# Block attention and feed-forward, one core: attn*v in three steps, scores ahead of transposes, raw keys of the last blocks turned a step earlier (batches 2 to 7)

## The chip, the cores and the metric

The program runs on one core of a Trainium2 chip. The metric is device time in microseconds (us), of which three runs are given for the kernel before. The profile is of one further execution. PE is the matmul engine, PEld its weight loads, DVE the vector engine, ACT the scalar engine, POOL GpSimd, SP the engine that issues the DMAs.

## The reference

For 8 batches, 8 heads, 576 positions and head size 64, attention with a block mask (block 64: a query sees its own and all earlier blocks); then the heads side by side as 4608 tokens of 512 go through two matrices with an activation between them.

```python
scores = scale * np.matmul(q, k.transpose(0, 1, 3, 2))
scores = np.where(block_i >= block_j, scores, -1e9)
attn = softmax(scores)              # over the keys
x = (attn @ v).transpose(0, 2, 1, 3).reshape(4608, 512)
h = x @ w_in                        # 512 -> 2048
g = np.where(h >= 1, h, np.where(h <= -1, 0, (h + 1) ** 2 / 4))
out = g @ w_out                     # 2048 -> 512
```

## The kernel before

Two heads of a batch make a pair; there are 32 pairs. `attention_steps` is a generator that writes out a pair in eight steps. From the 37th step on each attention step is followed by one half step of the feed-forward part: either `ffn_in` (12 matmuls of 512 columns into the bank `ph`, then four operations on ACT, DVE and POOL) or `ffn_out` (12 matmuls of 512 columns into the four banks `po`). Odd steps of a pair are followed by `ffn_out`, even ones by `ffn_in`. When attention is through, the feed-forward half steps that are left run alone.

PE takes its instructions in the order of the program, here as a scheduler has settled it; ACT, DVE, POOL and SP each have their own order, settled in the same way.

Pairs of batches 2 to 7 (24 of the 32) are "far" and "raw" in the code: their queries and keys come as they are and are split into two parts after the transpose, and much of a pair's work is done during the next pair's steps. Short names for the groups of matmuls, each of which fills one bank:

- S(j,g): scores of head j for one or two tiles of 128 queries, with 128 and 256 keys (g=0), 384 (g=1), 512 (g=2); method `scores`, lines 482 and 485. DVE takes the negated maximum of a row (L505), ACT the exponential and its sum (L509), DVE the inverse and the product (L491, L492, L515), and a DMA (`prr<-pr`) copies the result into a tile of another type, from which PE transposes it.
- SLa, SLb: the same for the last 64 queries of both heads, two banks of 4 matmuls of 288 columns (`scores_last`).
- T(j,g): transposes of that copy (L552 before, L565 after), 3 or 4 of 128 columns; ACT copies the bank (L545), DVE subtracts the copy from it (L547). TL is the same for the last 64 queries; its last 64 keys, the corner, have a bank of their own before the change (TLb).
- Q(j): four transposes of head j's raw queries and keys (`turned_raw`, L401), taken from the bank by ACT, DVE, ACT, DVE in turn. QL: one transpose for the last blocks of both heads (`turned_last`, L442), taken by ACT, DVE, ACT, DVE and two more on DVE.
- AF: attn*v of the first 256 positions of both heads (`attn_v_first`); A(j): of the other 320 positions of head j (`attn_v`); L591 before, L608 after. ACT copies one half to `xtmp` (L613), DVE adds the halves (L614).

All of these share three banks in turn (the pool `ps_w`): a group may start when the group three places before it has been taken out of its bank. The order of the groups before the change, for the steps 1 to 8 of a pair (names of the pair before it marked with '):

```
1: T(1,1)' S(0,0) AF'   2: T(1,2)' S(0,1) QL    3: A(1)' S(0,2)    4: T(0,0) SLa SLb
5: T(0,1) S(1,0) Q(0)   6: T(0,2) S(1,1)        7: TL TLb S(1,2)   8: T(1,0) A(0) Q(1)
```

Q(0) and Q(1) are those of the next pair, QL the pair's own.

Of the kernel before, what the change touches and what calls it, by code (L numbers as in the profile page):

```python
# [23 lines left out]
def block_attn_then_ffn(  # L24
# [230 lines left out]
    class Pair:  # L255
# [238 lines left out]
        def scores(self, j, g):  # L494
# [19 lines left out]
            for i, cs in enumerate(cols):  # L514
                nc.vector.tensor_scalar_mul(pr[:, cs], pr[:, cs], sm[:, i : i + 1])  # L515
            self.pr[j, g] = as_float32r(pr[:, : cols[-1].stop], self.plain) if self.hop else [pr]

        def scores_last(self):
# [22 lines left out]
            nc.vector.tensor_scalar_mul(pr, pr, sm[:, 2:3])  # L541
            self.pr["last"] = as_float32r(pr, self.plain) if self.hop else [pr]

# [27 lines left out]

        def turn_last(self):
            pr = self.pr.pop("last")
            ps = work_bank("ps_t")
            for c0 in range(0, SM, P):
# [4 lines left out]
            )  # L580
            ps = work_bank("ps_t")
            self.transposed(ps[:BLK, :P], pr, SM, BLK)
            self.split(
                ps[:BLK, :P].rearrange("p (h c) -> p h c", h=2), *(x[:BLK] for x in self.pc)
            )

# [44 lines left out]
        def attn_v_first(self):  # L631
            if self.plain:
                return self.both(0, self.parts_first)
            ps = work_bank("ps_av")
            for j in range(2):
                self.weighted(ps[:, j * G0 : (j + 1) * G0], j, self.parts_first(j))
            for j in range(2):
                self.add_halves(ps[:, j * G0 : (j + 1) * G0], j, 0)

        def attn_v(self, j):  # L640
# [3 lines left out]
            self.weighted(ps, j, self.parts(j))  # L644
            self.add_halves(ps, j, G0)

# [16 lines left out]
    def attention_steps():  # L663
# [10 lines left out]
        for i, cur in enumerate(pairs + [None]):  # L674
            nxt = pairs[i + 1] if i + 1 < len(pairs) else None
            far = old is not None and old.far
            near = old is not None and not old.far
            if far:
                old.turn(1, 1)
            if cur:  # L680
# [13 lines left out]
            if i + 2 < len(pairs):  # L694
                pairs[i + 2].fetch()
            if near:
                old.attn_v(1)
                old.store_x()
            yield
            if far:  # L700
                old.attn_v(1)
                old.store_x()
            if not cur:
                return
            if cur.far:
                cur.scores(0, 2)
            else:
                cur.begin()
                cur.scores(0, 2)
                cur.turn(0, 0)  # L710
            yield
            if cur.far:
                cur.begin()
                cur.turn(0, 0)
                cur.scores_last()
            else:
                cur.scores_last()
                cur.turn(0, 1)
            if nxt:
# [5 lines left out]
            if cur.far:  # L725
                cur.turn(0, 1)
                cur.scores(1, 0)
            else:
                cur.scores(1, 0)
                cur.turn(0, 2)  # L730
            if nxt:
                nxt.turned(True, 0)
            yield
            if cur.far:
                cur.turn(0, 2)
                cur.scores(1, 1)
            else:
                cur.scores(1, 1)
                cur.turn_last()
            if nxt:  # L740
                nxt.turned(False, 0)
            yield
            if cur.far:
                cur.turn_last()
                cur.scores(1, 2)
            else:
                cur.scores(1, 2)
                cur.attn_v(0)
                cur.turn(1, 0)
            yield  # L750
# [134 lines left out]
```

## Time and profile before

| | |
|---|---|
| median of 3 runs | 1267.78 us (1264.84 to 1269.26) |
| the profiled execution's own time | 1269.69 us |
| its span, first to last instruction | 1267.9 us |
| mean granted clock of TensorE | 0.981 of full speed |
| PE busy | 1200.1 us, 95% of the span |
| DVE, ACT, POOL busy | 70%, 55%, 31% |

Busy time is the union of what the records of an engine cover. The ends of matmuls are modelled and overlap the next one's start, so what a matmul costs is read from one start to the next, not from its length.

### The profile page before, as it was taken

Reading aid. Unit: us, or ns where it says so; the run is one execution under the profiler, and the core shown is the slowest. Engines: PE = TensorE matmul, PEld = TensorE weight load, DVE = VectorE, ACT = ScalarE, POOL = GpSimd, SP = SyncE. Lnnn points to the kernel's source line nnn. Section 1 sums busy time; section 2 is a strip of 40 time slices with the busy share of each in tenths; the row PEclk is TensorE's granted clock in tenths of the full one; section 3 lists DMA queues with packets and bytes.
Section 4 is the critical chain, followed back from the end, with each engine's and each line's share of the span. In section 5 each row is a group of like instructions: output and inputs, shape, how many; then the busy total and the mean of one; then the engine's idle time right before and its main releaser. Section 6 shows DMA issues by size and latency. Waiting matters only on the chain.

```text
span 1267.9 us, 20253 instructions
## 1 busy us (share of the span) xinstructions
PE 1200.1 (95%) x6280; PEld 998.8 (79%) x6280; DVE 887.0 (70%) x2188; ACT 703.2 (55%) x1827; POOL 394.6 (31%) x430
## 2 busy tenths in 40 slices
PE   5888889899999999999999999999999999999998
PEld 4666667678888888888888888888888888888886
DVE  8898877758777777777777777787777777322222
ACT  5787656646566655665656655566556555222222
POOL 3555655522222222222222222222222222222222
PEclk9888988999999999999999999999999999999999
DMA  5566666667888655555554655465556433422432
GB/s 158 167 176 215 203 228 197 217 198 237 260 273 266 215 162 158 154 175 163 156 162 145 187 157 152 138 189 153 160 154 190 137 128 118 132 87 98 133 100 100
DMA packets 185259, 215.43 MB, mean 170 GB/s; under 512 B 113840, under 2 KB 132272, under 8 KB 184384
## 3 DMA queue, kind: packets, MB, share of 16 engines
q1 hardware_dynamic: 185152, 214.14, 54.9%
q8 instruction: 50, 0.82, 0.3%
q14 instruction: 57, 0.47, 0.1%
HBM read 134.74 MB, written 31.98 MB: 131 GB/s over the span
## 4 chain that ended last, share of the span: by engine, by line
PE 69%; DVE 16%; ACT 6%; issue 5%; DMA 1%; POOL 1%; SPq 1%; ACTq 0%; POOLq 0%; DVEq 0%
PE ph L770 29%; PE po L794 15%; PE po L799 7%; PE ps_av L591 7%; PE ps_s L482 4%; ACT pr L509 3%; PE ps_s L485 3%; DVE t L780 2%; PE ps_t L552 2%; DVE t L783 2%; ACT t L779 2%; DVE pb L547 2%; DVE nm L505 2%; DVE sm L491 1%; DVE pr L515 1%
## 5 line engine op out<-in xcount | busy, mean ns | idle before, releaser
L785 POOL TENSOR_TENSOR gl<-t,gh 128x512 fp32r<-128x512 f32 x144 | 187.5, 1302 | 510.2 <-ACT gh L784 333.2
L794 PE MATMUL po<-wo,gh 128*128 128x512 f32 x1152 | 296.1, 397 | 0.5 <-DMA wo<-wo_split 0.3
L794 PEld LDWEIGHTS po<-wo,gh 128*128 128x128 f32 x1152 | 212.5, 189 | 44.5 <-DMA wo<-wo_split 0.7
L770 PE MATMUL ph<-xh,wih 128*128 128x512 f32 x576 | 232.9, 404 | 1.6 <-DVE t L783 1.6
L770 PE MATMUL ph<-xh,wil 128*128 128x512 f32 x576 | 228.8, 397 | 0.0
L770 PE MATMUL ph<-xl,wih 128*128 128x512 f32 x576 | 227.8, 396 | 0.5 <-DVE xl L627 0.5
L780 DVE SCALAR_TENSOR_TENSOR t<-t 128x512 f32<-128x512 f32 x144 | 101.5, 705 | 168.0 <-ACT t L779 165.2
L779 ACT ACTIVATE t<-ph 128x512 f32<-128x512 f32 x144 | 85.9, 597 | 173.8 <-PE ph L770 173.8
L509 ACT ACTIVATE pr<-ps_s,nm 128x128 f32<-128x128 f32 (+3 forms) x256 | 134.1, 527 | 60.5 <-DVE nm L505 58.4
L784 ACT CAST gh<-t 128x512 fp32r<-128x512 f32 x144 | 89.5, 621 | 120.3 <-DVE t L783 120.0
L799 PE MATMUL po<-wo,gl 128*128 128x512 f32 x576 | 155.6, 392 | 0.0
L482 PE MATMUL ps_s<-ka,qa 68*128 68x288 f32 (+4 forms) x384 | 135.3, 367 | 15.0 <-ACT pr L509 5.4
L379 POOL TENSOR_TENSOR vsr<-vn,vsr 128x256 fp32r<-128x256 f32 (+1 forms) x96 | 55.2, 576 | 246.2 <-ACT vsr L378 244.6
L770 PEld LDWEIGHTS ph<-xh,wil 128*128 128x128 f32 x576 | 109.5, 190 | 23.8
L770 PEld LDWEIGHTS ph<-xh,wih 128*128 128x128 f32 x576 | 109.8, 191 | 21.7 <-DVE t L783 2.3
L799 PEld LDWEIGHTS po<-wo,gl 128*128 128x128 f32 x576 | 108.7, 189 | 23.1
L505 DVE TENSOR_REDUCE nm<-ps_s 128x1 f32<-128x128 f32 (+3 forms) x256 | 118.8, 482 | 10.4 <-PE ps_s L485 9.4
L770 PEld LDWEIGHTS ph<-xl,wih 128*128 128x128 f32 x576 | 109.7, 190 | 20.5 <-DVE xl L627 0.9
L485 PE MATMUL ps_s<-kb,qb 128*128 128x288 f32 (+4 forms) x384 | 121.1, 322 | 0.0
L515 DVE TENSOR_SCALAR pr<-pr,sm 128x128 f32<-128x128 f32 (+3 forms) x256 | 107.3, 440 | 5.4
L783 DVE TENSOR_TENSOR t<-ph,t 128x512 f32<-128x512 f32 x144 | 98.7, 686 | 2.2
L491 DVE TENSOR_SCALAR sm<-sm 128x1 f32<-128x1 f32 (+1 forms) x224 | 52.0, 232 | 68.3 <-ACT pr L509 65.7
(111 smaller groups left out, 1871.4 us busy)
## 6 DMA issues: line engine op xcount, KB each, us to landing
wo<-wo_split SPq DMA_DIRECT2D x144, 512.0 KB, 3.5
prr<-pr SPq DMA_DIRECT2D x96, 192.0 KB, 2.5
prr<-pr SPq DMA_DIRECT2D x72, 256.0 KB, 2.8
out_dram<-ob SPq DMA_DIRECT2D x36, 256.0 KB, 2.9
bits<-in_moe_w_in_dram SPq DMA_DIRECT2D x32, 256.0 KB, 3.5
bits<-in_moe_w_out_dram SPq DMA_DIRECT2D x32, 256.0 KB, 3.0
wo_split<-ws SPq DMA_DIRECT2D x16, 512.0 KB, 2.9
qa<-qb SPq DMA_DIRECT2D x63, 128.0 KB, 2.4
```

Source lines behind the costliest of these rows:

```text
L482: nc.tensor.matmul(ps, qa[:KA, j, c0 : c0 + P], ka[:KA, j, k0 : k0 + n], start=first, stop=False)
L485: nc.tensor.matmul(ps, qb[:, j, c0 : c0 + P], kb[:, j, k0 : k0 + n], start=False, stop=last)
L505: nc.vector.tensor_reduce(out=nm[:, i : i + 1], in_=ps[:, cs], axis=AX.X, op=ALU.max, negate=True)
L509: nc.scalar.activation(pr[:, cs], ps[:, cs], AF.Exp, bias=nm[:, i : i + 1], scale=1.0, accum_out=sm[:, i : i + 1],)
L515: nc.vector.tensor_scalar_mul(pr[:, cs], pr[:, cs], sm[:, i : i + 1])
L770: nc.tensor.matmul(ph, w[:, cc, fs], x[:, cc, xs], start=(cc == 0 and i == 0), stop=(cc == NCC - 1 and i == 2),)
L779: nc.scalar.activation(t_, ph, AF.Relu, bias=0.5, scale=0.5)
L780: nc.vector.scalar_tensor_tensor(out=t_, in0=t_, scalar=1.0, in1=t_, op0=ALU.min, op1=ALU.mult)
L783: nc.vector.tensor_tensor(out=t_, in0=ph, in1=t_, op=ALU.max)
L785: nc.gpsimd.tensor_tensor(out=gl, in0=t_, in1=gh.bitcast(F32), op=ALU.subtract)
L794: nc.tensor.matmul(po[tt], gh[:, ts_], wo[:, w, :], start=(fc == 0 and w == 0), stop=False)
L799: nc.tensor.matmul(po[tt], gl[:, ts_], wo[:, 0, :], start=False, stop=fc == NFC - 1)
```

## The change

It concerns the far pairs alone. The order of the groups becomes

```
1: S(0,0) T(1,1)' A(0)'   2: S(0,1) T(1,2)' AF'   3: S(0,2) A(1)'        4: SLa SLb T(0,0)
5: S(1,0) T(0,1) Q(0)     6: S(1,1) T(0,2)        7: S(1,2) TL Q(1)      8: T(1,0)+corner QL
```

with QL now that of the next pair. Scores stand ahead of the transposes in a step; the three parts of attn*v are spread over steps 1, 2 and 3 of the next pair; the corner is transposed into the bank of T(1,0), so a pair has 21 groups instead of 22. The DMAs `prr<-pr` are written at the end of a step (`move`). In `add_halves` both halves of AF take their columns from one `xtmp` tile.

```diff
-            self.pr[j, g] = as_float32r(pr[:, : cols[-1].stop], self.plain) if self.hop else [pr]
+            self.pr[j, g] = [pr[:, : cols[-1].stop]]
+            if not self.far:
+                self.moved(j, g)
...
+        def move(self, *key):
+
+            if self.far:
+                self.moved(*key)
...
+            if self.far and j == 1 and g == 0:
+                self.turn_corner(self.pr.pop(("last",)), ps[:BLK, n : n + P])
...
-        def add_halves(self, ps, j, c0):
+        def add_halves(self, ps, j, c0, xtmp):
...
-            xtmp = att1.tile([P, G1], F32, tag="xtmp", name="xtmp")
...
+            xtmp = att1.tile([P, G1], F32, tag="xtmp", name="xtmp")
             for j in range(2):
-                self.add_halves(ps[:, j * G0 : (j + 1) * G0], j, 0)
+                self.add_halves(ps[:, j * G0 : (j + 1) * G0], j, 0, xtmp)
...
-            if far:
-                old.turn(1, 1)
             if cur:
                 cur.scores(0, 0)
                 cur.turned(False, 1)
                 cur.load("v")
             if far:
-                old.attn_v_first()
+                old.turn(1, 1)
+                old.attn_v(0)
...
+            if cur:
+                cur.scores(0, 1)
+                if not cur.raw:
+                    cur.turned_last()
...
             if far:
                 old.turn(1, 2)
-            if cur:
-                cur.scores(0, 1)
-                cur.turned_last()
+                old.attn_v_first()
...
             if far:
+                if cur:
+                    cur.scores(0, 2)
                 old.attn_v(1)
                 old.store_x()
...
             if cur.far:
                 cur.begin()
+                cur.scores_last()
                 cur.turn(0, 0)
-                cur.scores_last()
...
-            if cur.far:
-                cur.turn(0, 1)
-                cur.scores(1, 0)
+            cur.scores(1, 0)
+            cur.turn(0, 1 if cur.far else 2)
+            cur.move(1, 0)
...
+            cur.scores(1, 1)
             if cur.far:
                 cur.turn(0, 2)
-                cur.scores(1, 1)
...
+            cur.scores(1, 2)
             if cur.far:
                 cur.turn_last()
-                cur.scores(1, 2)
+                if nxt:
+                    nxt.turned(True, 1)
...
             if cur.far:
                 cur.turn(1, 0)
-                cur.attn_v(0)
...
+            if nxt and nxt.raw:
+                nxt.turned_last()
```

The first place is PE around step 2 of a pair in the middle of the program, before the change; L799 is the end of `ffn_out`, L770 the start of `ffn_in`.

```order
L799 MATMUL po<-wo,gl 128x512 x4
L552 MATMUL ps_t<-ident_r,prr 128x128 x4
L482 MATMUL ps_s<-ka,qa 128x384
L485 MATMUL ps_s<-kb,qb 128x384
L442 MATMUL ps_qk<-ident_r,qk 128x128
L770 MATMUL ph<-xh,wih 128x512
```

The same place after the change, where L828 is the end of `ffn_out`:

```order
L828 MATMUL po<-wo,gl 128x512 x4
L482 MATMUL ps_s<-ka,qa 128x384
L485 MATMUL ps_s<-kb,qb 128x384
L565 MATMUL ps_t<-ident_r,prr 128x128 x4
L608 MATMUL ps_av<-pa_6201,vsr_111 128x256
```

The single transpose L442 (QL), which stood behind S(0,1), is gone from this place; T(1,2)' has moved behind S(0,1), and AF' follows it.

The second place is PE from step 7 to the start of step 8 before the change; L794 and L799 are `ffn_out`.

```order
L552 MATMUL ps_t<-ident_r,prr 128x128 x4
L552 MATMUL ps_t<-ident_r,prr 64x128
L482 MATMUL ps_s<-ka,qa 128x512
L485 MATMUL ps_s<-kb,qb 128x512
L794 MATMUL po<-wo,gh 128x512 x8
L799 MATMUL po<-wo,gl 128x512 x4
L552 MATMUL ps_t<-ident_r,prr 128x128 x3
```

And after the change, as far as step 8's `ffn_in`:

```order
L482 MATMUL ps_s<-ka,qa 128x512
L485 MATMUL ps_s<-kb,qb 128x512
L565 MATMUL ps_t<-ident_r,prr 128x128 x4
L401 MATMUL ps_qk<-ident_r,qk 128x128 x4
L823 MATMUL po<-wo,gh 128x512 x8
L828 MATMUL po<-wo,gl 128x512 x4
L565 MATMUL ps_t<-ident_r,prr 128x128 x3
L565 MATMUL ps_t<-ident_r,prr 64x128
L442 MATMUL ps_qk<-ident_r,qk 128x128
```

S(1,2) now stands ahead of TL, as S(1,1) in step 6 of T(0,2); the corner (64x128) has moved from step 7 to step 8, Q(1) from step 8 to step 7, and QL has come to the end of step 8.

The third place is DVE behind step 4's `ffn_in` before the change: L780 and L783 are its two operations, L505 the maxima of S(1,0), L547 the part of T(0,1), L389 that of Q(0).

```order
L780 SCALAR_TENSOR_TENSOR t<-t 128x512
L547 TENSOR_TENSOR pb_7868<-ps_t,pb_7867 128x3x128
L783 TENSOR_TENSOR t<-ph,t 128x512
L505 TENSOR_REDUCE nm<-ps_s 128x1 x2
L389 SCALAR_TENSOR_TENSOR qb<-ps_qk,qb 64x512
L491 TENSOR_SCALAR sm<-sm 128x2
L492 RECIPROCAL sm<-sm 128x2
L515 TENSOR_SCALAR pr<-pr,sm 128x128
```

And after the change, with L809 and L812 for the two operations and L560 for T(0,1):

```order
L809 SCALAR_TENSOR_TENSOR t<-t 128x512
L505 TENSOR_REDUCE nm<-ps_s 128x1
L812 TENSOR_TENSOR t<-ph,t 128x512
L505 TENSOR_REDUCE nm<-ps_s 128x1
L560 TENSOR_TENSOR pb_7440<-ps_t,pb_7439 128x3x128
L389 SCALAR_TENSOR_TENSOR qb<-ps_qk,qb 64x512
L491 TENSOR_SCALAR sm<-sm 128x2
L492 RECIPROCAL sm<-sm 128x2
```

One of the two maxima of S(1,0) now stands between the two operations of `ffn_in`, and T(0,1)'s subtraction behind the other maximum.

## Rows read from the trace of the kernel before

**Rows 1.** The page, part 2: the granted clock in 40 slices.
```profile
PEclk9888988999999999999999999999999999999999
```

**Rows 2.** One pair's period: length, PE, PEld, DVE, ACT, POOL busy (records), clock, DMA.
```profile
704.49:737.90 33.41, 32.71 (x183) 27.83 (x183) 25.78 (x64) 19.87 (x54) 9.00 (x10) 1.00 0.53 157
```

**Rows 3.** All waits of PE in 311.8 to 1080 us: total, times, longest.
```profile
PE ps_qk L442 <- DVE x L614: 8.9, 23, 0.4
PE ps_s L482 <- ACT pr L509: 5.2, 17, 0.3
```

**Rows 4.** Line 442 (QL): lengths in ns, first and last start in us.
```profile
L442 PE MATMUL ps_qk<-ident_r,qk x24: 221/252/254, 274.4 to 1047.2; 128*128 128x128 f32 x24
```

**Rows 5.** PE in order of time, steps 1 to 2: start, length, instruction.
```profile
711.83 0.41 PE L482 MATMUL ps_s<-ka,qa 68*128 68x384 f32 x1
712.08 0.34 PE L485 MATMUL ps_s<-kb,qb 128*128 128x384 f32 x1
712.83 0.25 PE L442 MATMUL ps_qk<-ident_r,qk 128*128 128x128 f32 x1 [0.41 <-DVE x L614]
712.91 0.47 PE L770 MATMUL ph<-xh,wih 128*128 128x512 f32 x1
713.22 0.39 PE L770 MATMUL ph<-xl,wih 128*128 128x512 f32 x1
713.44 0.39 PE L770 MATMUL ph<-xh,wil 128*128 128x512 f32 x1
```

**Rows 6.** DVE and ACT before that wait, in order of time.
```profile
710.35 0.41 DVE L614 TENSOR_TENSOR x<-ps_av,xtmp 64x256 f32<-64x256 f32 x1
...
711.53 0.36 ACT L613 COPY xtmp<-ps_av 64x256 f32<-64x256 f32 x1
...
712.25 0.43 DVE L614 TENSOR_TENSOR x<-ps_av,xtmp 64x256 f32<-64x256 f32 x1
```

**Rows 7.** PE in order of time, steps 5 to 7.
```profile
724.32 0.37 PE L552 MATMUL ps_t<-ident_r,prr 128*128 128x128 f32 x3
...
728.18 0.45 PE L552 MATMUL ps_t<-ident_r,prr 128*128 128x128 f32 x4
728.49 0.45 PE L482 MATMUL ps_s<-ka,qa 68*128 68x384 f32 x1
728.78 0.34 PE L485 MATMUL ps_s<-kb,qb 128*128 128x384 f32 x1
728.96 0.39 PE L770 MATMUL ph<-xh,wih 128*128 128x512 f32 x1
...
731.71 0.51 PE L552 MATMUL ps_t<-ident_r,prr 128*128 128x128 f32 x5
732.51 0.50 PE L482 MATMUL ps_s<-ka,qa 68*128 68x512 f32 x1 [0.29 <-ACT pr L509]
732.85 0.40 PE L485 MATMUL ps_s<-kb,qb 128*128 128x512 f32 x1
```

**Rows 8.** DVE and ACT in order of time behind step 4.
```profile
724.57 0.60 ACT L779 ACTIVATE t<-ph 128x512 f32<-128x512 f32 x1 [0.82 <-PE ph L770]
...
725.81 0.55 DVE L547 TENSOR_TENSOR pb<-ps_t,pb 128x384 fp32r<-128x384 f32 x1
726.28 0.68 DVE L783 TENSOR_TENSOR t<-ph,t 128x512 f32<-128x512 f32 x1
...
727.00 0.62 ACT L784 CAST gh<-t 128x512 fp32r<-128x512 f32 x1 [0.86 <-DVE t L783]
...
728.24 0.20 ACT L509 ACTIVATION_READ_ACCUMULATOR pr<-ps_s,nm 128x1 f32 x1
```

**Rows 9.** Two of DVE's groups by form, one period: busy us, mean ns.
```profile
L395 DVE TENSOR_TENSOR kb<-ps_qk,kb 64x512 fp32r<-64x512 f32 x2 | 1.4, 692 | 0.7 <-ACT kb L394 0.6
...
L446 DVE TENSOR_SCALAR ka<-ps_qk 64x128 fp32r<-64x128 f32 x1 | 0.3, 293 | 0.0
```

**Rows 10.** Line 809: DVE's copies of finished output banks, lengths in ns.
```profile
L809 DVE COPY ob<-po x18: 678/686/692, 294.0 to 1262.9; 128x512 f32<-128x512 f32 x18
```

More of the change, by code (lines that the diff above doesn't have):

```diff
@@ L541, in scores_last @@
             nc.vector.tensor_scalar_mul(pr, pr, sm[:, 2:3])
-            self.pr["last"] = as_float32r(pr, self.plain) if self.hop else [pr]
+            self.pr["last",] = [pr]
+            if not self.far:
+                self.moved("last")
         def split(self, ps, hi, lo=None):
@@ L572, in turn_last @@
         def turn_last(self):
-            pr = self.pr.pop("last")
+            pr = self.pr["last",] if self.far else self.pr.pop(("last",))
             ps = work_bank("ps_t")
@@ L580, in turn_last, with turn_corner @@
             )
[L581 to L585, printed above, removed]
+            if not self.far:
+                self.turn_corner(pr, work_bank("ps_t")[:BLK, :P])
+        def turn_corner(self, pr, ps):
+            self.transposed(ps, pr, SM, BLK)
+            self.split(ps.rearrange("p (h c) -> p h c", h=2), *(x[:BLK] for x in self.pc))
         def weighted(self, ps, j, parts, first=True, last=True):
@@ L644, in attn_v @@
             self.weighted(ps, j, self.parts(j))
-            self.add_halves(ps, j, G0)
+            self.add_halves(ps, j, G0, att1.tile([P, G1], F32, tag="xtmp", name="xtmp"))
         def store_x(self):
@@ L684, in attention_steps @@
             if far:
-                old.attn_v_first()
+                old.turn(1, 1)
+                old.attn_v(0)
             if near:
                 old.turn(1, 2)
+            if cur:
+                cur.move(0, 0)
             yield
+            if cur:
+                cur.scores(0, 1)
+                if not cur.raw:
+                    cur.turned_last()
+            if i + 2 < len(pairs):
+                pairs[i + 2].fetch()
             if far:
                 old.turn(1, 2)
-            if cur:
-                cur.scores(0, 1)
-                cur.turned_last()
-            if i + 2 < len(pairs):
-                pairs[i + 2].fetch()
+                old.attn_v_first()
             if near:
@@ L698, in attention_steps @@
                 old.store_x()
+            if cur:
+                cur.move(0, 1)
             yield
             if far:
+                if cur:
+                    cur.scores(0, 2)
                 old.attn_v(1)
                 old.store_x()
-            if not cur:
-                return
-            if cur.far:
+                if not cur:
+                    return
+                if not cur.far:
+                    cur.begin()
+                    cur.turn(0, 0)
+            elif cur.far:
                 cur.scores(0, 2)
@@ L710, in attention_steps @@
                 cur.turn(0, 0)
+            cur.move(0, 2)
             yield
@@ L718, in attention_steps @@
                 cur.turn(0, 1)
+            cur.move("last")
             if nxt:
@@ L733, in attention_steps @@
             yield
+            cur.scores(1, 1)
             if cur.far:
                 cur.turn(0, 2)
-                cur.scores(1, 1)
             else:
-                cur.scores(1, 1)
                 cur.turn_last()
+            cur.move(1, 1)
             if nxt:
@@ L742, in attention_steps @@
             yield
+            cur.scores(1, 2)
             if cur.far:
                 cur.turn_last()
-                cur.scores(1, 2)
+                if nxt:
+                    nxt.turned(True, 1)
             else:
-                cur.scores(1, 2)
                 cur.attn_v(0)
                 cur.turn(1, 0)
+            cur.move(1, 2)
             yield
@@ L756, in attention_steps @@
                 cur.attn_v_first()
-            if nxt:
+            if nxt and not cur.far:
                 nxt.turned(True, 1)
+            if nxt and nxt.raw:
+                nxt.turned_last()
             yield
```

7 lines of the change are left out of this document (3 added, 4 removed).

## The prediction

> **What bounds the kernel now.** I looked first at the granted clock: from the eighth of 40 slices on it is nine tenths or more [rows 1], and in a far pair 1.00, the upper level, 2.4 GHz [rows 2], so nothing is to be had from the clock where the change acts. Then at such a pair, one whole period: 33.41 us long, with PE covered for 32.71, DVE for 25.78, ACT for 19.87 [rows 2]. PE is the bound, and the view of waits shows what it still waits for. Between 311.8 and 1080 us there are two waits and no others: QL for DVE's addition of the halves of AF (23 times), and S(1,2) for ACT's exponential (17 times) [rows 3]. QL runs 24 times from 274.4 to 1047.2 us [rows 4], 23 periods of 33.6 us on average, so both waits repeat in nearly every pair.
>
> Because the ends of matmuls are modelled, I take each wait's cost from starts. The second matmul of S(0,1) starts at 712.08 and QL at 712.83, 0.75 us apart [rows 5]; where nothing waits, the same matmul of 384 columns takes 0.18 (728.78 to 728.96) [rows 7]. So QL's wait costs 0.57, not the recorded 0.41. TL and TLb, five transposes, start at 731.71 and S(1,2) at 732.51: 0.80; four transposes take 0.31 (728.18 to 728.49), five thus 0.39 [rows 7]. S(1,2)'s wait costs 0.41.
>
> Both are waits for one of the three banks. QL follows AF by three groups; AF needs two copies and two additions, one after the other, and the second addition runs from 712.25 to 712.68 because its copy came only at 711.53, behind an exponential [rows 6]. S(1,2) follows S(1,1) by three groups, because TL has a second bank.
>
> **What the change does, part by part.** *QL away from AF, corner away from step 7.* QL now has TL three places before it, S(1,2) has Q(0), two steps back. Both waits lose their reason. 23 x 0.57 = 13.1 us and 17 x 0.41 = 7.0 us. What comes three groups behind AF is now SLa, two steps later; three groups behind S(1,1) comes TL, which starts a whole `ffn_in` (2.75 us from 728.96 to 731.71 [rows 7]) and two groups after it.
>
> *Scores ahead of transposes.* Behind short matmuls a first long one pays for its weights: the 512 columns of S(1,2) take 0.34 (732.51 to 732.85) and the 384 of S(1,1) 0.29 (728.49 to 728.78) [rows 7], where 512 columns in a row take 0.22 (713.22 to 713.44) [rows 5] and 384 take 0.18. That is 0.11 to 0.12 each. Before, seven scores of a pair (all but SLb) stood behind transposes or attn*v; after, none does: -0.8. On the other side `ffn` now comes behind short matmuls in all eight steps instead of four (AF, QL, Q(0), Q(1)), at 0.09 each (712.91 to 713.22 is 0.31 against 0.22 [rows 5]): +0.36. A(0)' and AF' both stand behind transposes now, where one did, and the short scores of g=0 gain less than the long ones: together an estimate of +0.2 from the same rows. Left: about -0.2 per pair; bounds 0 and -0.3. 24 x 0.2 = 4.8 us.
>
> The Trainium skill (TensorE: Matmul & The Clock Gate, "Step-by-step: what each phase is for") says that the next tile's weights are loaded while this tile's matmul runs. By that rule the order of scores and transposes would be worth nothing and the sum would lack the 4.8 us. The trace shows the load uncovered behind short matmuls, so I go by the rows.
>
> *A wait that I expect in place of another.* S(1,1) needs the bank of S(1,0), which is taken behind step 4's `ffn_in`: ACT's `t` at 724.57, DVE's second operation at 726.28, ACT's `gh` at 727.00, then the exponentials, whose last piece ends at 728.44 (728.24 plus 0.20) [rows 8]. S(1,1) started at 728.49 [rows 7]: a tie, because T(0,2) stood in front of it for 0.31. Now S(1,1) wants to start when `ffn_out` ends, at 728.18 on this scale, 3.86 after the step's start at 724.32. On DVE the subtraction of T(0,1) no longer stands ahead of the second operation, but one maximum does: 0.28 for 0.47 (725.81 to 726.28), so the exponentials end about 0.2 earlier, at 728.25. With the passing of the signal and a weight load that then lies open, S(1,1) comes 0.1 to 0.3 late; I take 0.2 (bounds 0, if the maxima run earlier than I think, and 0.4, if the exponentials end as before and the load lies open). Queued behind it on PE are T(0,2) and the `ffn_in` of step 6, so it is paid in full. 24 x 0.2 = +4.8 us.
>
> *A(0)' behind QL, AF' behind A(0)'.* A(0)' wants its bank 7.8 us after S(1,2) starts (0.46, 0.3, 0.3, an `ffn_out` and an `ffn_in` of 2.8 each, 0.4, 0.5 and 0.2 between them). Until QL is taken DVE has 15 operations in a row, from S(1,2)'s maximum to QL's last: six of 512 columns at 0.69, seven small ones at 0.29 or less [rows 9], two in between at about 0.5, so 7.1 us by recorded lengths, from 0.7 on, plus 0.3 for a hand-over: 8.1. But lengths overlap: 0.55 recorded is 0.47 from start to start (725.81 to 726.28 [rows 8]), which takes off about 0.07 each, 1 us. It fits by some tenths; I take 0, bounds 0 and 0.35. AF' needs A(0)' taken: one copy and one addition (0.43 [rows 6]) where AF had two of each, and S(0,1) and T(1,2)' stand between. I take 0 as well.
>
> *The copies of finished output.* In every fourth pair DVE has two copies of 0.69 [rows 10] behind step 5. They can come ahead of S(1,1)'s maximum, and TL waits for S(1,1) now. TL wants its bank an `ffn_in` and two groups, 3.5 us, after S(1,1); in this time DVE has to end S(1,0) and Q(0) and take the maximum, which leaves about half a microsecond. Five such pairs: bounds 0 and 1.4 each (all of both copies); I take 0.5, +2.5 us.
>
> *Nothing.* The later writing of the DMAs `prr<-pr`: each copy is used about three steps, over 10 us, after it is issued, and so it stays off the path; without that cover the `wo` and `qk` loads queued behind on SP would be late. QL at the end of step 8 frees step 2's place and adds one transpose to step 8, the same work. One `xtmp` for both halves saves a wait in AF that nobody waits for any more.
>
> **The sum.** -13.1 - 7.0 - 4.8 + 4.8 + 2.5 = -17.6 us. The profiled execution took 1269.69 us (span 1267.9 and 1.8 around it), 1.9 above the median of 1267.78; so 1252.1 for it and 1250.2 for the median. I say 1250.
>
> **The rivals.**
>
> *All waits vanish.* S(1,0)'s exponentials end in time and nothing replaces the two waits: bounds of each term, -13.1 - 7.0 - 7.2 = -27.3, some 1241 us. For it: DVE has 7.6 us free in a period. Against: the tie at 728.44 and 728.49. Chance 0.13.
>
> *The wait moves.* With three banks and a period whose slack lies elsewhere, S(1,1) waits 0.4, A(0)' 0.35 and TL in five pairs 1.4: -13.1 - 7.0 - 4.8 + 9.6 + 8.4 + 7.0 = +0.1, so 1260 to 1268 us. For it: the row of 15 on DVE has no gap. Chance 0.17, half of it within 0.3%.
>
> *Slower.* That same row of DVE runs late in every pair, since Q(1), the corner, T(1,0) and QL all come out in turns of ACT and DVE. Then A(0)' waits, with `ffn_out`, S(0,1) and AF' behind it on PE. It decides from 21.4/24 = 0.9 us per pair (17.6 and the 0.3%); at 1.2 us, the time is 1250 + 29 = 1279. Against: it needs three times the upper bound that I found. Chance 0.08.
>
> *Not what it says.* If QL's wait were for something other than AF's bank, the term of 13.1 would move with QL to step 8. The releaser is DVE's addition each time [rows 3], which speaks against it. It lies in the second rival's chance.
>
> **How the numbers follow.** The forecast has 0.60, at 1244 to 1258 us; the rule on weights alone would give 1255, inside it. The range of 8 in 10 reaches to the first rival and into the second: 1241 to 1263. A measurement of this kernel can tell about 0.3%, 3.8 us, from no change: faster means under 1264. Faster 0.60 + 0.13 + 0.08 and a little of the rest, 0.82; same 0.10; slower 0.08.
>
> **What would show it.** Right: QL and S(1,2) gone from PE's waits; a period of 32.5 to 32.8 us between QL's starts; first score matmuls of 512 columns at 0.22 to 0.25; S(1,1) waiting a tenth or three for ACT's exponential. Wrong: A(0)' or T(1,1)' waiting for DVE (the row of 15), TL waiting in every pair, or a period above 33.2 us.

## The result, and the profile after

| | median | runs |
|---|---|---|
| before | 1267.47 us | 14 (1264.18 to 1269.6) |
| after | 1269.51 us | 14 (1267.96 to 1272.79) |

The ratio is 1.0023, 95% interval 1.0013 to 1.0032: the changed kernel is no faster, 2 us slower if anything, and the 17.6 us forecast did not come. The profiled execution took 1270.94 us, its span is 1269.1.

Four pairs in a row, a whole chunk of the feed-forward part with its output copies, from one QL to the fourth after it. The columns are those of [rows 2]. After:

```profile
669.59:803.55 133.96, 131.05 (x731) 112.22 (x730) 110.15 (x254) 80.70 (x210) 36.17 (x40) 1.00 0.54 162
```

And before:

```profile
646.08:779.74 133.66, 131.22 (x729) 111.21 (x729) 103.39 (x255) 79.97 (x208) 35.82 (x38) 1.00 0.54 162
```

A pair takes 33.49 us after and 33.41 before (133.96 and 133.66, by four). PE does as much as it did. DVE is busy 6.76 us longer with one operation fewer: some of its operations have become longer, and the rest follows from one of them.

PE's waits of more than 0.15 us between 315 and 1030 us after; before, over 311.8 to 1080 us, these were [rows 3]:

```profile
PE ps_av L608 <- DVE ka L446: 11.5, 21, 0.6
PE ps_t L565 <- DVE pb L560: 1.9, 5, 0.4
```

Both old waits are gone. A new one is larger than QL's was (11.5 us in 21 pairs; before, 8.9 in 23): A(0)' (L608) waits for DVE to take QL (L446). The other is at TL, in the five pairs with output copies, as I expected; but TL waits for DVE's taking of T(0,2) there, not of S(1,1).

PE at QL, S(0,0), T(1,1)' and A(0)', after:

```profile
736.85 0.23 PE L442 MATMUL ps_qk<-ident_r,qk 128*128 128x128 f32 x1
...
740.09 0.28 PE L485 MATMUL ps_s<-kb,qb 128*128 128x256 f32 x1
740.44 0.42 PE L565 MATMUL ps_t<-ident_r,prr 128*128 128x128 f32 x3
741.41 0.82 PE L608 MATMUL ps_av<-pb,vsr 128*128 128x320 f32 x4 [0.55 <-DVE ka L446]
```

A(0)' starts 0.97 behind T(1,1)', whose three transposes take 0.23 where nothing waits (728.92 to 729.15 in the experiment with the product on GpSimd, below). T(1,1)' itself starts 0.35 behind the last matmul of S(0,0), there 0.13 (728.79 to 728.92). So this pair loses 0.74 and 0.22, 0.96 us (on average over 21 pairs 0.98), where before a pair lost 0.57 at QL and, in 17 of 24, 0.41 at S(1,2) [rows 5, 7].

The cause stands in the same stretch on DVE, with GpSimd's one operation below:

```profile
733.36 0.68 DVE L505 TENSOR_REDUCE nm<-ps_s 128x1 f32<-128x512 f32 x1
...
736.84 1.35 DVE L515 TENSOR_SCALAR pr<-pr,sm 128x512 f32<-128x512 f32 x1
738.23 0.69 DVE L395 TENSOR_TENSOR kb<-ps_qk,kb 64x512 fp32r<-64x512 f32 x1
...
739.78 0.56 DVE L560 TENSOR_TENSOR pa<-ps_t,pa 128x384 fp32r<-128x384 f32 x1 [0.23 <-ACT pa L558]
...
740.97 0.29 DVE L446 TENSOR_SCALAR ka<-ps_qk 64x128 fp32r<-64x128 f32 x1
...
736.62 1.29 POOL L814 TENSOR_TENSOR gl<-t,gh 128x512 fp32r<-128x512 f32 x1 [6.85 <-ACT gh L813]
```

The product of S(1,2) (L515) takes 1.35. It starts 0.22 behind GpSimd's gl and ends 0.28 behind gl's end (738.19 and 737.91). What follows it in the row is late by that: T(1,1)' needs the bank of T(1,0), which DVE leaves at 740.34 (`pa`), and A(0)' that of QL, which it leaves at 741.26 (`ka`). Some of DVE's groups by form, 333 to 1040 us after (busy us, mean ns of one; half of the products of 512 columns are S(0,2)'s, which start ahead of gl):

```profile
L515 DVE TENSOR_SCALAR pr<-pr,sm 128x512 f32<-128x512 f32 x43 | 37.6, 874 | 1.4
...
L515 DVE TENSOR_SCALAR pr<-pr,sm 128x384 f32<-128x384 f32 x42 | 27.1, 644 | 1.7 <-DVE sm L492 0.3
...
L491 DVE TENSOR_SCALAR sm<-sm 128x2 f32<-128x2 f32 x42 | 24.6, 585 | 15.5 <-ACT pr L509 14.8
...
L491 DVE TENSOR_SCALAR sm<-sm 128x1 f32<-128x1 f32 x106 | 15.7, 148 | 1.7
...
L544 DVE TENSOR_TENSOR nm<-nm 128x1 f32<-128x1 f32 x21 | 11.8, 560 | 0.7
```

and before:

```profile
L515 DVE TENSOR_SCALAR pr<-pr,sm 128x512 f32<-128x512 f32 x43 | 21.2, 494 | 1.5
L491 DVE TENSOR_SCALAR sm<-sm 128x2 f32<-128x2 f32 x42 | 21.0, 500 | 20.5 <-ACT pr L509 20.5
...
L515 DVE TENSOR_SCALAR pr<-pr,sm 128x384 f32<-128x384 f32 x42 | 17.6, 420 | 1.3
...
L533 DVE TENSOR_TENSOR nm<-nm 128x1 f32<-128x1 f32 x21 | 3.3, 159 | 0.7
```

DVE's products of 512 columns are dearer by 380 ns on average in after. The two-column sum looks dear in both, 500 and 585 against 148 for one column; with gl off GpSimd (experiment 6) it is 169. The product of S(1,2) is somewhat under half of what DVE lost (16.4 of the 38 us by which these four groups grew). The others are half of the products of 384 columns, those of S(0,1), 0.88 beside another subtraction of GpSimd (`vsr`), the two-column sums, and a minimum of one column (L533 before, L544 after), whose two inputs both lie in SBUF. The view of PE's waits names none of these.

The Trainium skill (SBUF — State Buffer, "Who interferes with whom") says that a `tensor_scalar` of VectorE in a two-port mode and a GpSimd operation exclude each other, the one that comes later being blocked until the other has ended. The Trainium skill (VectorE: DVE Perf Modes, "Mode 2×_2P") says that this mode wants its operands in SBUF and an outermost dimension, of those larger than one, that is even, or odd and the same in source and destination. The trace agrees so far as it goes: 512 columns and two columns from SBUF are held up, the sum of one column is not, and what DVE takes out of PSUM keeps its length beside GpSimd (Q(1)'s `kb` of 512 columns takes 0.69 beside gl in experiment 5, at 725.97, and without gl in experiment 1; a copy of finished output takes 0.69 wholly under gl in before, at 427.67, and 0.68 to 0.69 without gl in experiment 2).

### The profile page after: what moved, and what is told of

Read it like the earlier page. It is cut to its first block, busy times and chain, and to the rows that moved or that the text cites. A ratio compares the mean times of both kernels' runs of the same rounds, so it can differ in the third digit from the quotient of the medians.

```text
span 1269.1 us, 20236 instructions
## 1 busy us (share of the span) xinstructions
PE 1197.7 (94%) x6280; PEld 1003.9 (79%) x6280; DVE 933.3 (74%) x2188; ACT 704.3 (55%) x1827; POOL 394.7 (31%) x430
## 4 chain that ended last, share of the span: by engine, by line
PE 57%; DVE 27%; issue 4%; ACT 4%; DMA 3%; POOL 2%; SPq 1%; ACTq 0%; POOLq 0%; DVEq 0%
PE ph L799 19%; PE po L823 14%; PE ps_av L608 9%; PE po L828 7%; DVE pr L515 4%; DVE nm L505 3%; DVE kb L395 3%; PE ps_s L482 3%; PE ps_s L485 3%; DVE pb L560 2%; DVE t L809 2%; DVE t L812 2%; DVE qb L389 2%; PE ps_t L565 2%; POOL work L183 1%
## 5 line engine op out<-in xcount | busy, mean ns | idle before, releaser
L814 POOL TENSOR_TENSOR gl<-t,gh 128x512 fp32r<-128x512 f32 x144 | 192.7, 1338 | 605.9 <-ACT gh L813 430.1
L823 PEld LDWEIGHTS po<-wo,gh 128*128 128x128 f32 x1152 | 208.0, 188 | 40.6 <-DMA wo<-wo_split 1.2
L799 PE MATMUL ph<-xh,wih 128*128 128x512 f32 x576 | 236.2, 410 | 1.7 <-DVE t L812 1.6
L799 PE MATMUL ph<-xl,wih 128*128 128x512 f32 x576 | 227.3, 395 | 0.8 <-DVE xl L643 0.8
L799 PE MATMUL ph<-xh,wil 128*128 128x512 f32 x576 | 226.9, 394 | 0.0
L809 DVE SCALAR_TENSOR_TENSOR t<-t 128x512 f32<-128x512 f32 x144 | 101.6, 706 | 148.8 <-ACT t L808 147.0
L828 PE MATMUL po<-wo,gl 128*128 128x512 f32 x576 | 155.0, 391 | 0.0
L505 DVE TENSOR_REDUCE nm<-ps_s 128x1 f32<-128x128 f32 (+3 forms) x256 | 123.7, 486 | 26.8 <-PE ps_s L485 23.5
L515 DVE TENSOR_SCALAR pr<-pr,sm 128x128 f32<-128x128 f32 (+3 forms) x256 | 135.2, 548 | 5.1 <-DVE sm L492 0.3
L482 PE MATMUL ps_s<-ka,qa 68*128 68x288 f32 (+4 forms) x384 | 123.4, 336 | 8.9 <-ACT kb L427 4.1
L799 PEld LDWEIGHTS ph<-xh,wil 128*128 128x128 f32 x576 | 109.3, 190 | 24.3
L799 PEld LDWEIGHTS ph<-xh,wih 128*128 128x128 f32 x576 | 109.2, 189 | 21.9 <-DVE t L812 2.5
L828 PEld LDWEIGHTS po<-wo,gl 128*128 128x128 f32 x576 | 108.1, 188 | 22.8
L799 PEld LDWEIGHTS ph<-xl,wih 128*128 128x128 f32 x576 | 109.7, 190 | 20.7 <-DVE xl L643 1.4
L812 DVE TENSOR_TENSOR t<-ph,t 128x512 f32<-128x512 f32 x144 | 98.6, 685 | 2.0
L379 POOL TENSOR_TENSOR vsr<-vn,vsr 128x256 fp32r<-128x256 f32 (+1 forms) x96 | 50.6, 528 | 149.0 <-ACT vsr L378 147.7
L558 ACT CAST pb<-ps_t 128x512 fp32r<-128x512 f32 (+1 forms) x120 | 65.4, 545 | 47.5 <-PE ps_t L565 45.1
```

The source lines that it names most:

```text
L482: nc.tensor.matmul(ps, qa[:KA, j, c0 : c0 + P], ka[:KA, j, k0 : k0 + n], start=first, stop=False)
L505: nc.vector.tensor_reduce(out=nm[:, i : i + 1], in_=ps[:, cs], axis=AX.X, op=ALU.max, negate=True)
L799: nc.tensor.matmul(ph, w[:, cc, fs], x[:, cc, xs], start=(cc == 0 and i == 0), stop=(cc == NCC - 1 and i == 2),)
L809: nc.vector.scalar_tensor_tensor(out=t_, in0=t_, scalar=1.0, in1=t_, op0=ALU.min, op1=ALU.mult)
L812: nc.vector.tensor_tensor(out=t_, in0=ph, in1=t_, op=ALU.max)
L814: nc.gpsimd.tensor_tensor(out=gl, in0=t_, in1=gh.bitcast(F32), op=ALU.subtract)
```

## The experiments

Two theories. **P**: the product of S(1,2) waits for gl, and that makes the row of DVE ahead of A(0)' too long. **R**: the row of 15 operations is too long by itself. The table's fourth column is the time of a pair over four pairs; the fifth the time from QL's start until DVE has ended `ka`, median of some 20 pairs. Where nothing waits, A(0)' starts 3.59 behind QL (725.56 to 729.15 in experiment 5).

| kernel | median | ratio to before | us a pair | QL taken |
|---|---|---|---|---|
| after | 1269.51 | 1.0023 (1.0013 to 1.0032) | 33.49 | 4.42 |
| 1 no gl | 1243.76 | 0.9818 (0.9799 to 0.9837) | 32.61 | 3.49 |
| 2 before, no gl | 1247.06 | 0.9854 (0.9839 to 0.9868) | 32.71 | |
| 3 product on ACT | 1257.07 | 0.9931 (0.9910 to 0.9952) | 32.96 | 3.75 |
| 4 QL taken by ACT | 1269.59 | 1.0023 (1.0011 to 1.0036) | 33.46 | 4.42 |
| 5 product on GpSimd | 1251.17 | 0.9881 (0.9853 to 0.9909) | 32.67 | 3.45 |
| 6 gl on DVE | 1256.24 | 0.9921 (0.9901 to 0.9942) | 33.01 | 3.96 |
| 7 no gl, transposes first | 1253.83 | 0.9903 (0.9880 to 0.9926) | 33.13 | 3.92 |
| 8 gl in halves | 1264.17 | 0.9982 (0.9970 to 0.9993) | 33.27 | 4.02 |
| 9 before, product on GpSimd | 1268.37 | 1.0008 (0.9997 to 1.0018) | 33.42 | |
| 10 as 5, copies on ACT | 1248.46 | 0.9849 (0.9829 to 0.9870) | 32.47 | 3.45 |
| 11 before, single sums | 1250.22 | 0.9863 (0.9845 to 0.9881) | 32.75 | |
| 12 as 10, single sums | 1240.17 | 0.9793 (0.9770 to 0.9815) | 32.44 | 3.39 |
| 13 after, single sums | 1264.04 | 0.9964 (0.9951 to 0.9976) | 33.38 | 4.36 |
| 14 before, single sums, copies on ACT | 1247.70 | 0.9842 (0.9829 to 0.9856) | 32.74 | |

### 1 and 2: gl left out, in both kernels

```diff
-        gl = ffn.tile([P, TCH], F32R, tag="gl", name="gl")
+        gl = gh
...
-        nc.gpsimd.tensor_tensor(out=gl, in0=t_, in1=gh.bitcast(F32), op=ALU.subtract)
```

> The changed kernel with GpSimd's subtraction gl left out; the matmuls that take gl take gh in its place, so PE does the same work and the output lacks the low part of the activation. Theory P (DVE's product of S(1,2), 1.35 us instead of 0.49, waits for GpSimd's gl, and this lengthens the row of DVE operations in front of A(0)'): the product takes 0.49, A(0)' waits under 0.2 us, a pair takes 32.5 to 32.7 us, 1250 to 1255 us in all. Theory R (the row of 15 DVE operations is too long by itself, and GpSimd has no part in it): A(0)' still waits 0.5 to 0.7, 1266 to 1271 us.

> The kernel before with the same piece left out (gl's subtraction; gh in its place). Theory P: the additions on two columns of sums (0.50 us each, twice a pair) fall to 0.16, AF's second addition comes 0.35 earlier and QL's wait falls from 0.57 to about 0.2: 1255 to 1262 us. Theory R: no change, 1265 to 1269 us.

DVE of the first: the maximum of S(1,2), its product, the end of QL's taking.

```profile
716.98 0.69 DVE L505 TENSOR_REDUCE nm<-ps_s 128x1 f32<-128x512 f32 x1 [0.32 <-PE ps_s L485]
...
720.48 0.49 DVE L515 TENSOR_SCALAR pr<-pr,sm 128x512 f32<-128x512 f32 x1
...
723.74 0.29 DVE L446 TENSOR_SCALAR ka<-ps_qk 64x128 fp32r<-64x128 f32 x1
```

The row runs from 716.98 to 724.03, 7.05 us, which is what I had added up (7.1); in after it runs from 733.36 to 741.26, 7.90. R falls. But before gains as much from the same edit, 20 us, and the view of waits shows none left in it: its two waits were mainly GpSimd's work too. Both kernels came out below the ranges that I had given for P. R keeps a small share: in the five pairs with output copies A(0)' still waits up to 0.5 without gl (2.3 us in all). And in before a part of QL's wait is left: QL still starts 0.39 behind S(0,1)'s second matmul (731.11 to 731.50), where 0.18 is free [rows 7], and its load starts 0.12 behind AF's second addition, with gl as without. Without gl the change is worth 3.3 us (1247.06 and 1243.76); the last experiment comes back to this.

### 3 and 4: other engines for the product, and for the end of QL

```diff
-                nc.vector.tensor_scalar_mul(pr[:, cs], pr[:, cs], sm[:, i : i + 1])
+                if self.far and (j, g) == (1, 2):
+                    nc.scalar.activation(pr[:, cs], pr[:, cs], AF.Copy, scale=sm[:, i : i + 1])
+                else:
+                    nc.vector.tensor_scalar_mul(pr[:, cs], pr[:, cs], sm[:, i : i + 1])
```

> The changed kernel with the product of S(1,2) alone made on ACT instead of DVE, in the far pairs. Theory P: DVE's row loses 1.35 us of which 0.86 was waiting, A(0)' waits 0.1 or nothing, a pair takes 32.5 to 32.8 us, 1250 to 1256 us. Theory R: the row loses the 0.4 us that the product takes by itself, A(0)' still waits 0.3, 1259 to 1263 us.

The fourth has `nc.scalar.mul` for `qa` and `ka` of QL (L446) instead.

> The changed kernel with the last two operations of QL (qa and ka, 0.29 each) on ACT instead of DVE. Both theories: QL's bank comes free some 0.5 us earlier, A(0)' waits 0.1 to 0.3 instead of 0.73; T(1,1)' keeps its 0.24, since T(1,0) is taken before it. 1257 to 1262 us. If neither moves, the releaser that the trace names is not the one, 1268 to 1271 us.

The third gains 12.4 us on after, a microsecond above P's range. What stays is ACT's own time: its product (726.21, 0.73 long) stands ahead of its copy of the corner (`pcs`, 726.96), for which DVE waits 0.34.

The fourth is a miss: two operations fewer on DVE, and nothing gained. On ACT `pa` waits 1.59 for the corner's subtraction on DVE, behind the long product, and `qa` 0.67 for DVE's `kb`. QL is taken 4.42 behind its start, as in after: the chain alternates between ACT and DVE, so shortening its end on one engine does not move it. What counts is what stands ahead.

### 5, 6 and 8: gl and the product kept apart, with nothing left out

The fifth has `nc.gpsimd` in place of the third's ACT product, the sixth `nc.vector` for gl, the eighth gl in two GpSimd instructions of 256 columns.

> After, with one edit: the product of S(1,2) is GpSimd's, behind its own gl, instead of DVE's. Nothing is left out. If the product's waiting for gl is what makes A(0)' late (theory P), DVE's row loses 1.35 us there and nothing on DVE waits for GpSimd between QL's taking and A(0)'; A(0)' wants its bank 0.73 earlier than it gets it in after, so its wait goes, the period falls by about 0.9 to 32.5 us, and the time is 1245 to 1252 us. If the row of DVE is too long by itself (theory R), it becomes shorter by the free length of 0.49 alone: A(0)' still waits 0.2, time 1256 to 1260.

> After, with gl subtracted by DVE instead of GpSimd, in all half steps. Nothing is left out. In the row before A(0)' one more operation of 0.69 then stands right ahead of the product. Theory P: the product takes its free 0.49 again, so the two take 1.18 where the product took 1.35 alone; A(0)' waits 0.5 to 0.6 instead of 0.73, DVE's sums and products elsewhere are at their free lengths (0.15 and 0.49), time 1258 to 1267. Theory R: the row gets 0.69 longer, A(0)' waits 1.4, time 1283 to 1288.

> After, with gl subtracted by GpSimd in two instructions of 256 columns instead of one of 512. Nothing is left out. Theory P: a DVE operation that waits for GpSimd can start between the halves, so the product of S(1,2) takes about 0.9 instead of 1.35, A(0)' waits 0.4 less, time 1258 to 1263; if GpSimd keeps DVE out over both halves, the product is as long as in after or longer and the time that of after, 1269 to 1272. Theory R: no change, 1269 to 1271, with the product's length not mattering.

The fifth: PE, the last DVE operation on QL, and GpSimd.

```profile
725.56 0.23 PE L442 MATMUL ps_qk<-ident_r,qk 128*128 128x128 f32 x1
...
728.79 0.28 PE L485 MATMUL ps_s<-kb,qb 128*128 128x256 f32 x1
728.92 0.37 PE L568 MATMUL ps_t<-ident_r,prr 128*128 128x128 f32 x3
729.15 1.12 PE L611 MATMUL ps_av<-pb,vsr 128*128 128x320 f32 x6
...
728.71 0.29 DVE L446 TENSOR_SCALAR ka<-ps_qk 64x128 fp32r<-64x128 f32 x1
...
725.33 1.29 POOL L817 TENSOR_TENSOR gl<-t,gh 128x512 fp32r<-128x512 f32 x1 [6.85 <-ACT gh L816]
726.60 1.57 POOL L516 TENSOR_SCALAR pr<-pr,sm 128x512 f32<-128x512 f32 x1
```

A(0)' waits no more outside the five pairs with output copies (1.7 us in all there); GpSimd's product takes 1.57, and nobody needs it before step 2 of the next pair. The sixth, DVE:

```profile
727.00 0.67 DVE L814 TENSOR_TENSOR gl<-t,gh 128x512 fp32r<-128x512 f32 x1
727.59 0.48 DVE L515 TENSOR_SCALAR pr<-pr,sm 128x512 f32<-128x512 f32 x1
...
730.85 0.29 DVE L446 TENSOR_SCALAR ka<-ps_qk 64x128 fp32r<-64x128 f32 x1
```

Here the row has one operation *more* and A(0)' comes earlier: gl and the product take 1.07 from start to end (727.00 to 728.07) where the product alone took 1.35. R expected 1283 to 1288; it is 13 us faster than after, which is also more than P gave it. (Not all of DVE's products are at their free lengths, as I had expected: S(0,1)'s is still 0.88 beside `vsr`.) The eighth: DVE's product, and GpSimd's two halves as one row.

```profile
733.99 0.81 DVE L515 TENSOR_SCALAR pr<-pr,sm 128x512 f32<-128x512 f32 x1
...
733.77 1.63 POOL L816 TENSOR_TENSOR gl<-t,gh 128x256 fp32r<-128x256 f32 x2 [6.86 <-PE po L832]
```

The product gets in between the halves, 0.81 long; QL is taken 0.40 earlier and a pair is 0.22 shorter (1264.17 us, just above P's range of 1258 to 1263). Over kernels 1, 3, 5, 6, 8 and 13 the pair gets shorter, to within 0.2 us, by as much as QL is taken earlier, whatever the means. P stands.

### 7: is the order of scores and transposes worth anything?

The first experiment's kernel with the transposes ahead of the scores again.

> The kernel of the first experiment (after, gl's subtraction left out) with the transposes ahead of the scores again in steps 1, 2 and 4 to 7, and A(1)' ahead of S(0,2) in step 3; the banks are used in that order. gl is left out here as there. It tells what scores ahead of transposes are worth where GpSimd disturbs nothing. The prediction's term: 0.2 us per pair, 24 pairs, so 1248 to 1249 us against 1243.8. The starts of the trace of after say about nothing, because feed-forward matmuls behind short ones pay the load back: 1243 to 1245. A new wait for a bank would show as such in PE's waits and is then to be taken off.

It is 0.52 us a pair slower, but nearly all by two new waits. PE:

```profile
725.73 0.43 PE L565 MATMUL ps_t<-ident_r,prr 128*128 128x128 f32 x4
726.24 0.28 PE L442 MATMUL ps_qk<-ident_r,qk 128*128 128x128 f32 x1
...
729.78 0.28 PE L485 MATMUL ps_s<-kb,qb 128*128 128x256 f32 x1
730.31 0.38 PE L608 MATMUL ps_av<-pb,vsr 128*128 128x320 f32 x1 [0.24 <-DVE ka L446]
```

Four transposes and then QL take 0.51, in the first kernel 0.27 (720.27 to 720.54 there): QL waits 0.24 for the exponential of S(1,2). S(0,0)'s last matmul to A(0)' is 0.53, of which the matmul is 0.13 (728.79 to 728.92 in the fifth): 0.4 more. Over some 20 pairs the two are 0.21 and 0.41 on average; but the first experiment's kernel has waits of 0.17 of its own at A(0)', so that 0.45 of the 0.48 by which these pairs are longer are waits. Some 0.05 us a pair is left for the order itself.

### 9, 11 and 13: what held the kernel before

DVE, ACT and GpSimd before, at the places of its two waits:

```profile
711.53 0.49 DVE L491 TENSOR_SCALAR sm<-sm 128x2 f32<-128x2 f32 x1 [0.78 <-ACT pr L509]
...
728.47 0.59 DVE L491 TENSOR_SCALAR sm<-sm 128x2 f32<-128x2 f32 x1 [0.27 <-ACT pr L509]
...
731.21 0.55 DVE L505 TENSOR_REDUCE nm<-ps_s 128x1 f32<-128x384 f32 x1
...
731.79 0.58 ACT L509 ACTIVATE pr<-ps_s,nm 128x384 f32<-128x384 f32 x1 [2.13 <-DVE nm L505]
...
710.70 1.29 POOL L785 TENSOR_TENSOR gl<-t,gh 128x512 fp32r<-128x512 f32 x1 [0.99 <-ACT gh L784]
...
727.75 1.29 POOL L785 TENSOR_TENSOR gl<-t,gh 128x512 fp32r<-128x512 f32 x1 [6.20 <-issue]
```

Behind S(0,0)'s exponentials the two-column sum runs until gl ends (712.02 and 711.99), and the second addition of AF, for which QL waits, stands behind it at 712.25 [rows 6]. Behind S(1,0)'s the same sum ends with gl (729.06 and 729.04), and behind it stand the maximum and the exponential of S(1,1), for which S(1,2) waits.

```diff
-            self.inverse(sm[:, :m])
+            for i in range(m):
+                nc.vector.tensor_scalar_add(sm[:, i : i + 1], sm[:, i : i + 1], EPS)
+            nc.vector.reciprocal(sm[:, :m], sm[:, :m])
```

> Before, with the edit that gained most in after: the product of S(1,2) is GpSimd's. Nothing is left out. Theory P says it is a matter of which operation stands beside gl: in before that product comes right behind gl and takes its free 0.49 already, and what stands under gl is the sum of S(0,0), ahead of the second addition of AF. So QL waits as before and the time is 1263 to 1268 us. If less work on DVE is worth the same wherever it is taken off, it falls by 10 to 15 us as in after, to 1252 to 1257.

> Before, with the addition of the small constant to the two sums of S(0,0) and S(1,0) done in two operations of one column, which are 0.15 us with and without GpSimd running, instead of one of two columns, 0.49 under gl. Nothing is left out. Theory P for QL's wait in before: the second addition of AF comes 0.15 to 0.2 earlier, so QL does, 23 times: 1262 to 1265 us, and QL starts about 0.58 behind S(0,1)'s second matmul instead of 0.75. If AF's addition is held by something else, no change: 1266 to 1269.

> After, with the sums of S(0,0) and S(1,0) in operations of one column, the edit that took 17 us off before. Nothing is left out. Theory P, with the product of S(1,2) as the only thing that makes A(0)' late in after: the far pairs stay as they are (period 33.26 to 33.45, A(0)' waiting 11 to 12 us in all), and what is gained lies ahead of them, some 10 us as between the two kernels with the product on GpSimd (where the first QL came 9.6 us earlier): 1258 to 1262 us. If these sums are part of A(0)'s wait, its total falls to 6 us or less and the time to 1243 to 1253.

The ninth shows that it is a matter of which operation meets gl: the edit worth 18 us in after is worth nothing in before. The eleventh gains 17.7 us, far more than I expected. DVE and GpSimd:

```profile
698.38 0.15 DVE L514 TENSOR_SCALAR sm<-sm 128x1 f32<-128x1 f32 x1 [0.32 <-ACT pr L509]
698.84 0.15 DVE L514 TENSOR_SCALAR sm<-sm 128x1 f32<-128x1 f32 x1 [0.30 <-ACT pr L509]
...
699.23 0.43 DVE L616 TENSOR_TENSOR x<-ps_av,xtmp 64x256 f32<-64x256 f32 x1
...
698.01 1.29 POOL L787 TENSOR_TENSOR gl<-t,gh 128x512 fp32r<-128x512 f32 x1 [0.99 <-ACT gh L786]
```

One-column sums take 0.15 under gl, and the first is done while the second exponential still runs, which I had not counted; QL starts 0.41 behind S(0,1)'s second matmul (699.39 to 699.80) instead of 0.75. And S(1,2)'s wait went with it, of which I had not thought. One more instruction at each of these sums gives the 17 us that the reordering was forecast to give. In the thirteenth the same edit leaves A(0)'s wait in after as it is (11.5 us in 21 cases, again): there the sums do not hold A(0)'. It gains 5.5 us, less than the 7.5 to 11.5 expected.

### 10, 12 and 14: the best version, and the change's own worth

The tenth is the fifth with ACT for DVE's copies of finished output (`ob<-po`), the twelfth has the single sums as well.

> After with the product of S(1,2) on GpSimd, and DVE's two copies of finished output (every fourth pair) on ACT too. Nothing is left out. If these copies make the pairs at a chunk's end longer (32.9 to 33.0 us instead of 32.41 in two of four periods, with TL and A(0)' waiting for DVE), the longer periods shrink to about 32.5 and the time is 1245 to 1248 us. If the length comes from something else there, it stays at 1250 to 1252.

> The kernel with the product of S(1,2) on GpSimd and the copies on ACT, and with the sums in operations of one column as well. Nothing is left out. DVE's wait for gl at these sums goes (0.59 for two columns to 0.15 twice), but PE waits for nothing behind them any more, so the time stays within 2 us of the kernel without it; 3 us or more faster would say that a wait is left that the profile does not name.

> Before, with the sums in operations of one column and the copies of finished output on ACT: the same cures that the fastest version of after has, so far as before needs them. Nothing is left out. It tells what the change itself is worth where GpSimd no longer sets the end. If the rest of QL's wait (0.2 us per pair) and the order of scores are all that is left, before takes 1247 to 1250 us with a period of 32.70, against 1240.2 and 32.37: the change is worth 7 to 10 us of the 17.6 forecast. If the change is worth nothing by itself, before comes to 1239 to 1242 as well.

Four pairs of the twelfth, and then of the fourteenth:

```profile
651.61:781.36 129.75, 129.66 (x731) 112.02 (x730) 102.29 (x256) 81.29 (x212) 42.30 (x44) 1.00 0.55 167
```

```profile
664.80:795.75 130.95, 130.74 (x729) 111.29 (x729) 101.80 (x261) 81.27 (x212) 35.84 (x39) 1.00 0.56 165
```

PE is covered for all but 0.09 of 129.75 us, and the view of waits shows none in the far pairs. The twelfth is the fastest kernel, 2.1% under before. It is 8.3 us faster than the tenth, where I expected at most 2; by my own words a wait was left that the profile does not name, and it is not in the far pairs, which differ by 0.03 us each. Against before with the cures that it needs it is 7.5 us faster by the medians (1240.17 and 1247.70), 6 by the two ratios, and 0.30 us a pair (1.20 by four, 24 pairs 7.2 us): that is what the change is worth. By the starts most of it is what is left of QL's wait, though no run takes that away by itself: in the fourteenth QL starts 0.40 behind S(0,1)'s second matmul (729.83 to 730.23), 0.22 more than the free 0.18. Without gl the change was worth less, 0.10 us a pair, with the output copies still on DVE, where they cost after more than before.

## Why the prediction was wrong

*The two waits: right as waits, wrong as causes.* QL and S(1,2) no longer wait, -20.1 us as worked out. But I took the bank three places back for the reason. It is the place; the length of the chain that empties it came from gl, and a change of place alone leaves that as it is.

*A(0)' behind QL, "I take 0, bounds 0 and 0.35": the step that failed.* It cost 0.74, and 0.22 at T(1,1)', which needs the bank of T(1,0) out of the same row: 0.96 by 24 is 23 us, and this took back what the two waits gave. Two things in the sum of that row were wrong.

The first is a length. I added the row up with lengths at which nothing ran on GpSimd; the product "at about 0.5" took 1.35. Before, S(1,2) stood behind TL, and its product came as gl ended (737.17, gl 735.88 to 737.17); with S(1,2) ahead of TL it comes just after gl has begun. The bound should have been taken from the two-column sums, in which the trace of before had the same stretch: 500 ns on average for an operation that takes 150 in one column.

The second is the overlap. I took off 1 us, 0.07 for each of 15 operations, and so found some tenths to spare. Without gl (experiment 1) the row takes 7.05 from start to end, and its recorded lengths add up to 6.88: the long operations do overlap, but gaps use that up (0.23 ahead of `pa`). With its start 0.67 behind S(1,2), A(0)' comes 7.87 behind it (716.31 to 724.18), and I had it wanting its bank at 7.8. So there was nothing to spare, and what gl added was paid nearly in full.

The second rival named the row, but gave it the same lengths. The slower one asked for 0.9 us a pair, and 0.96 came: that rival is what happened, though the time stayed within the 0.3%. With it the forecast of -17.6 would have been +5.4; +2.0 was measured.

*Scores ahead of transposes, -4.8: little.* The first matmul of a score is 0.23 to 0.24 now (732.62 to 732.86), as forecast, but `ffn` behind short matmuls in all eight steps pays most of it back: the seventh experiment leaves 0.05 us a pair, and between the fourteenth and the twelfth some 0.08 is left beside QL's rest, for the order and all else, so 1 to 2 us in all. The rule of the Trainium skill against which I weighed it (TensorE: Matmul & The Clock Gate, "Step-by-step: what each phase is for") would have been nearly right on this term. The loads do lie open even so, as the rows of the prediction show (0.31 to 0.34 against 0.22).

*S(1,1) waits for S(1,0)'s exponential, +4.8: no wait, because it takes another bank.* S(1,1)'s first weight load and matmul, and ACT, after:

```profile
728.90 0.19 PEld L482 LDWEIGHTS ps_s<-ka,qa 68*128 68x128 f32 x1
729.13 0.35 PE L482 MATMUL ps_s<-ka,qa 68*128 68x384 f32 x1
...
728.60 0.47 ACT L509 ACTIVATE pr<-ps_s,nm 128x256 f32<-128x256 f32 x1
728.96 0.20 ACT L509 ACTIVATION_READ_ACCUMULATOR pr<-ps_s,nm 128x1 f32 x1
```

And ACT ahead of S(1,2), which waits, before:

```profile
732.27 0.19 ACT L509 ACTIVATION_READ_ACCUMULATOR pr<-ps_s,nm 128x1 f32 x1
```

It is the load that waits for the bank. Before, S(1,2) starts at 732.51 [rows 7], 0.05 behind the end of the read of the sum (732.46), and S(1,1) at 728.49, 0.05 behind its own (728.44): so what I called a tie was a wait. After, S(1,1)'s load starts at 728.90, 0.16 ahead of the end of the exponential (728.60 plus 0.47). In the trace it waits for a semaphore that DVE's instructions raise, and before, S(1,1)'s for one that ACT's raise. So the bank is not that of S(1,0). By these semaphores it is that of T(0,1), which DVE has left at 728.48, and T(0,2) takes S(1,0)'s. "The group three places before it" is therefore no fixed rule in this kernel: neighbours can be exchanged, as at TL in the pairs with output copies.

*The output copies, +2.5: about right.* In after the pair with them takes 33.89 us (669.59 to 703.48), the other three 33.36 on average: 0.53 by five pairs is 2.7 us. The fifth against the tenth has 2.7 us for them too by the medians (1251.17 and 1248.46), but 0.20 us a pair, 4.8 in 24, by the fourth column of the table.

*The sum.* With what the rows show, a pair should change by -0.57 for QL, -0.31 for S(1,2) (0.41 in three of four pairs), +0.96, and +0.13 for the copies (a quarter of 0.53), which is +0.21 us; the four pairs show +0.08. The order of the scores accounts for 0.05 to 0.08 of the difference; the rest stays open.

*Open.* What the sums cost ahead of the far pairs. Between the tenth and the twelfth the first QL comes 10.6 us earlier, between after and the thirteenth 3.9. But kernels that are alike up to there (after, 3, 4, 5 and 10) have it anywhere from 264.1 to 271.1 us in their profiles, so one trace of each cannot tell, and the 9.6 us on which my expectation of the thirteenth rests is no measure.

## What to carry to other kernels

Before adding up a row of DVE operations, mark those that will run while GpSimd does, and take their lengths from such a place; a two-column operation at three times the price of one column has already told it. When a wait goes away by moving work, ask what the moved row now runs beside, not only what it runs behind. And look for the disturbance first: one instruction that did not meet GpSimd was worth more here than the whole reordering.

## What the runs showed of the hardware

- DVE's `TENSOR_SCALAR` from SBUF to SBUF that starts under a GpSimd subtraction of 1.29 us ends just behind it, by 0.02 to 0.28: 512 columns 1.35 instead of 0.49, two columns 0.49 to 0.59 instead of 0.17. A `TENSOR_SCALAR` of one column takes 0.15 either way, and subtractions and copies out of PSUM keep their lengths. A minimum of two one-column tiles, both in SBUF (`TENSOR_TENSOR`), is held up too: 560 ns on average in after, 159 in before.
- Of the product and gl, whichever starts first goes on: in after a product of DVE starts at 720.23 and takes its 0.49, and gl, at 720.31, takes 1.56 instead of 1.29. With gl in two halves the product got in between them, 0.81.
- Where PE waits for the bank of an exponential, it gets it with the end of the read of ACT's accumulated sum, not of the exponential: S(1,2) starts 0.05 behind that read in before (732.46, 732.51), QL in the seventh experiment likewise (726.19, 726.24).
